# Second copies of 19 weight tiles, shared keys in the first products with v, normalizing on GpSimd

## The chip, the cores and the metric

The kernel runs on one core of a Trainium2 chip. A time is the device time of one execution in microseconds. The kernel before was timed three times: 958.98, 959.74 and 959.84 us, median 959.74.

The engines of a core are called here as in the profile: PE is TensorE (matmuls; PEld are its weight loads), DVE is VectorE, ACT is ScalarE, POOL is GpSimd, SP is SyncE, on whose queue this kernel issues all its transfers.

## The reference

```python
def _attn_ref(q, k, v):                  # each [8, 8, 576, 64], float32
    scores = matmul(q, k.T) / sqrt(64)
    rel = pos[:, None] - pos[None, :]
    mask_plain = (rel >= 0) & (rel < 32)                      # heads 0 to 3
    mask_dil = (rel >= 0) & (rel < 128) & (rel % 4 == 0)      # heads 4 to 7
    scores = where(mask, scores, -1e9)
    attn = exp(scores - max(scores))
    attn = attn / (sum(attn) + 1e-09)
    return matmul(attn, v)

def _moe_ref(x, w_in, w_out):            # [4608, 512], [512, 2048], [2048, 512]
    h = x @ w_in
    g = 0.5 * h * (1 + erf(h / sqrt(2)))
    return g @ w_out
```

x is the attention's result with a token's eight heads side by side. The weights reach the kernel as float64, the rest as float32.

## The kernel before, in words

**Tiling.** The 8 x 576 tokens are 16 chunks of 288 (`HALF`), half a batch entry each. Of a chunk, attention goes by four pairs of two heads: pairs 0 and 1 are plain, 2 and 3 dilated. The FFN follows with `h(c, f)`, the first product of chunk c for the f-th 128 of the 2048 hidden columns (`ffn_h`, L434, 12 matmuls of 288 columns), Gelu on ACT (L438), the split of g into a high and a low part (L441 on ACT, L443 on DVE), and the second product `o` (`ffn_o`, L448, 12 matmuls per f).

**Attention of a pair.** `scores` multiplies blocks of 32 queries with 64 keys each (L317). A dilated pair is laid out by residue of the position modulo 4, so its four row groups of 32 partitions hold one residue each, 72 queries in three blocks of 24 (computed 32 wide). A plain pair has three row groups. `lowest` adds the mask and finds the extremum (L329), `softmax` takes the exponential with its sum (L337; from chunk 2 on in other steps, `less`, `wide` and `sums`), `norm` divides by the sum (L357 to L366), `turn` transposes 32x32 squares (L374, and L379 from chunk 2 on), `av` multiplies with v (L403), and `xout` takes the result out of PSUM into a high part x (ACT, L421) and a low part (DVE subtraction, L423).

**Products with v.** In chunks 0 and 1 the 64 keys of a block are two halves of 32, a product of 32 rows each, added up in PSUM: 36 products for a plain pair, 48 for a dilated one. From chunk 2 on `turn` puts the two halves under each other, and one product has 64 rows; there are 18 and 24. A float32 product is two matmul records in the trace.

**Weights.** A tile of w_in or w_out is 128x512 float64, 512 KB, with the low word of each number first (`raw[:, :, 0]`) and the high word second. DVE splits it by integer passes. L243 shifts the low word right by 9, L245 ors the high word's last 9 bits on top (the low part's significand), L205 and L207 form a float32 from the high word (the high part, cut to 12 significand bits by the mask; ACT copies it, L217), L211 takes its exponent, and L255 multiplies the two to the low part. L205, L243 and L211 read one tile, the others two. The first tile is joined in another way (`w_join`, `w_join_pe`): TensorE adds the full value and minus the high part in PSUM (L233 to L235, with `ident` and `units`), and ACT copies the rest out (L237).

**Order.** Attention of chunks 0 to 2, all 32 weight tiles and the FFN of chunks 0 and 1 are ordered by `Plan`. It is a list scheduler that runs while the program is written: each job names what it comes after, which buffers it takes and gives back (`rings`), its rank and the guessed duration of each step, and the job that can start first is written next, with ranks for ties. The order that it writes is the order in each engine's queue. From chunk 3 on the attention steps stand at fixed places between the FFN's matmuls (`A_LOAD` to `A_N`, L598). Gelu of chunk 0 starts after all exponentials of chunk 1. Chunk 2's exponentials come after h(1, 15). The ring `wo` has 17 buffers for raw weight tiles, finished w_out tiles, and the keys and v of chunks 0 and 1.

Of the kernel before, what the change touches and what calls it, by code (L numbers as in the profile page):

```python
# [133 lines left out]
def attn_ffn(ctx: ExitStack, tc: tile.TileContext, qk_p, qk_d, v_p, v_d, w_in, w_out, outT):  # L134
# [28 lines left out]
    for k, d in ((PLAIN, KB), (DILATED, 2 * KB - QR)):  # L163
        for r in range(4):
            select(k, k, r, d, -1, 1, ALU.is_ge)
            select(k, k, r, WIN - d, 1, -1, ALU.is_gt)
        if k == PLAIN:
            select(PLAIN0, PLAIN, None, 0, 1, 0, ALU.is_ge)
            select(PLAIN0, PLAIN0, 0, -KB, 1, 0, ALU.is_ge)
            ident = const.tile([P, P], F32, name="ident")  # L170
            make_identity(nc, ident)
    select(DILATED0, DILATED, None, QR - 2 * KB, 1, 0, ALU.is_ge)
    select(DILATED1, DILATED, None, 2 * QR - 2 * KB, 1, 0, ALU.is_ge)
# [12 lines left out]
    units = []  # L186

    def w_units():

        yield {"DVE": 0.4}  # L190
        units.append(work.tile([P, 2, P], F32R, tag="go", name="units", bufs=3))
        for t, u in enumerate((1.0, -1.0)):
            nc.vector.tensor_scalar_mul(units[0][:, t], ident, u)
# [25 lines left out]
    def w_join(s, dst, i):  # L219

        raw = s["raw"]
        yield from w_top(s, 0x3FFFFFF8, gpool, "g", NF + 2)
        yield from w_exp(s)
        yield {"DVE": 0.6}
        g = s["g"] = gpool.tile([P, DM], F32R, tag="g", name="gw")
        nc.vector.scalar_tensor_tensor(g, raw[:, :, 0], 2.0 ** -52, raw[:, :, 1].bitcast(F32),
                                       op0=ALU.mult, op1=ALU.mult)

    def w_join_pe(s, dst, i):
        h, l = dst[i][:, 0], dst[i][:, 1]  # L230
        yield {"PE": 1.5}
        ps = ps_m.tile([P, 512], F32, tag="m", name="ps_w")
        nc.tensor.matmul(ps, ident, s["f"].bitcast(F32), start=True, stop=False)  # L233
        nc.tensor.matmul(ps, units[0][:, 1], h, start=False, stop=False)
        nc.tensor.matmul(ps, units[0][:, 0], s["g"], start=False, stop=True)  # L235
        yield {"ACT": 0.49}
        nc.scalar.copy(l, ps)  # L237
# [470 lines left out]
```

## Time and profile before

| | |
|---|---|
| median of three runs | 959.74 us |
| profiled execution, its own time | 960.52 us |
| its span | 958.7 us |
| mean granted TensorE clock | 0.982 |
| PE busy | 926.3 us (97%) |
| DVE busy | 486.9 us (51%) |
| ACT busy | 435.0 us (45%) |
| POOL busy | 6.2 us (1%) |
| DMA | 74.80 MB, mean 78 GB/s |

The page also has the span in 40 equal slices of some 24 us. A digit is the busy share of a slice in tenths:

```profile
PE   4589999999999999999999999999999999999998
DVE  6889996463533536244463534536353353634420
ACT  4644443554625345362443636245462534536240
POOL 2000000000000000000000000000000000000000
PEclk9589999999999999999999999999999999999999
DMA  9833323313040220403022040211304022040000
```

An idle engine is only worth something where another one waits for it, so the slices are read for the engine that is full, and the chain of waits for what it waited for. "issue" in the trace stands for time in which an engine waited for nothing that the profile shows.

### The profile page before, as it was taken

Reading aid. Unit: us, or ns where it says so; the run is one execution under the profiler, and the core shown is the slowest. Engines: PE = TensorE matmul, PEld = TensorE weight load, DVE = VectorE, ACT = ScalarE, POOL = GpSimd, SP = SyncE. Lnnn points to the kernel's source line nnn. Section 1 sums busy time; section 2 is a strip of 40 time slices with the busy share of each in tenths; the row PEclk is TensorE's granted clock in tenths of the full one; section 3 lists DMA queues with packets and bytes.
Section 4 is the critical chain, followed back from the end, with each engine's and each line's share of the span. In section 5 each row is a group of like instructions: output and inputs, shape, how many; then the busy total and the mean of one; then the engine's idle time right before and its main releaser. Section 6 shows DMA issues by size and latency. Waiting matters only on the chain.

```text
span 958.7 us, 27831 instructions
## 1 busy us (share of the span) xinstructions
PE 926.3 (97%) x11860; PEld 906.8 (95%) x11860; DVE 486.9 (51%) x1800; ACT 435.0 (45%) x1385; POOL 6.2 (1%) x27
## 2 busy tenths in 40 slices
PE   4589999999999999999999999999999999999998
PEld 2479999999999999999999999999999999999998
DVE  6889996463533536244463534536353353634420
ACT  4644443554625345362443636245462534536240
POOL 2000000000000000000000000000000000000000
PEclk9589999999999999999999999999999999999999
DMA  9833323313040220403022040211304022040000
GB/s 297 297 116 111 94 84 121 121 46 106 8 144 1 78 74 11 140 9 129 17 77 75 8 143 2 92 60 44 107 8 144 2 78 73 14 138 8 20 1 25
DMA packets 32252, 74.80 MB, mean 78 GB/s; under 512 B 3584, under 2 KB 11776, under 8 KB 32128
## 3 DMA queue, kind: packets, MB, share of 16 engines
q1 hardware_dynamic: 32128, 73.02, 23.1%
q8 instruction: 93, 1.52, 0.7%
q14 instruction: 31, 0.25, 0.1%
HBM read 63.57 MB, written 9.44 MB: 76 GB/s over the span
## 4 chain that ended last, share of the span: by engine, by line
PE 89%; DVE 7%; issue 2%; DMA 2%; SPq 0%; ACT 0%
PE ps_o L448 40%; PE ps_h L434 40%; PE px_a L403 4%; PE ps_a L317 3%; DVE cv L207 1%; DVE raw_w L245 1%; PE px L403 1%; DMA raw_qk<-qk_p 1%; DVE g L443 1%; DMA raw_qk<-qk_d 1%; PE ps_sc L317 1%; DVE raw_w L243 1%; DVE wout L255 1%; DVE cv L205 1%; DVE raw_w L211 1%
## 5 line engine op out<-in xcount | busy, mean ns | idle before, releaser
L448 PE MATMUL ps_o<-g,wout 128*128 128x288 f32 x3072 | 421.9, 296 | 0.9 <-DVE g L443 0.8
L448 PEld LDWEIGHTS ps_o<-g,wout 128*128 128x128 f32 x3072 | 410.4, 188 | 2.9 <-DVE g L443 1.7
L434 PE MATMUL ps_h<-xh,win 128*128 128x288 f32 x1920 | 390.5, 298 | 0.0
L434 PEld LDWEIGHTS ps_h<-xh,win 128*128 128x128 f32 x1920 | 308.8, 189 | 5.8 <-issue 3.2
L434 PE MATMUL ps_h<-xl,win 128*128 128x288 f32 x960 | 283.2, 295 | 0.0
L443 DVE TENSOR_TENSOR g<-gf,g 128x288 fp32r<-128x288 f32 x256 | 116.9, 457 | 261.5 <-ACT g L441 261.5
L438 ACT ACTIVATE gf<-ps_h 128x288 f32<-128x288 f32 x256 | 105.4, 412 | 293.1 <-PE ps_h L434 289.3
L434 PEld LDWEIGHTS ps_h<-xl,win 128*128 128x128 f32 x960 | 181.7, 189 | 0.0
L337 ACT ACTIVATE sm<-sm,st 96x64 f32<-96x64 f32 (+1 forms) x360 | 119.9, 334 | 14.4 <-DVE st L329 14.2
L441 ACT CAST g<-gf 128x288 fp32r<-128x288 f32 x256 | 110.7, 432 | 8.0
L421 ACT CAST xh<-px_a 128x288 fp32r<-128x288 f32 x52 | 27.8, 535 | 141.0 <-PE px_a L403 112.3
L379 DVE STREAM_TRANSPOSE turned<-sm 32x192 f32<-32x192 f32 x196 | 72.4, 369 | 5.3
L183 DVE COPY o_sb<-ps_o 128x288 f32<-128x288 f32 x58 | 26.4, 456 | 84.1 <-PE ps_o L448 82.0
L337 ACT ACTIVATION_READ_ACCUMULATOR sm<-sm,st 96x1 f32 (+1 forms) x360 | 67.4, 187 | 0.0
L423 DVE TENSOR_TENSOR xl<-px_a,xh 128x288 fp32r<-128x288 f32 x52 | 29.4, 565 | 58.5 <-ACT xh L421 58.1
L329 DVE CUSTOM_DVE_ANT_0 sm<-ps_a,masks 96x64 f32<-96x64 f32 (+1 forms) x312 | 46.9, 218 | 0.0
L403 PEld LDWEIGHTS px_a<-turned,v_all 64*64 64x64 f32 x2184 | 38.6, 134 | 4.2 <-issue 4.2
L403 PE MATMUL px_a<-turned,v_all 64*64 64x24 f32 (+1 forms) x2184 | 41.4, 218 | 0.0
L374 DVE STREAM_TRANSPOSE turned<-sm 96x384 f32<-96x384 f32 (+1 forms) x64 | 36.8, 575 | 2.0
L366 DVE TENSOR_TENSOR sm<-sm,st 96x384 f32<-96x384 f32 (+1 forms) x62 | 34.4, 555 | 1.8
L329 DVE DVE_READ_ACCUMULATOR2_ANT st<- 96x1 f32 (+1 forms) x384 | 30.9, 81 | 0.0
L317 PE MATMUL ps_sc<-raw_qk 64*32 64x64 f32 x504 | 11.3, 285 | 20.2 <-issue 9.9
(50 smaller groups left out, 377.1 us busy)
## 6 DMA issues: line engine op xcount, KB each, us to landing
raw_qk<-qk_d SPq DMA_DIRECT2D x32, 368.0 KB, 5.5
v_all<-v_p SPq DMA_DIRECT2D x28, 384.0 KB, 4.1
v_all<-v_d SPq DMA_DIRECT2D x28, 384.0 KB, 5.6
raw_qk<-qk_p SPq DMA_DIRECT2D x32, 304.0 KB, 3.5
outT<-o_sb SPq DMA_DIRECT2D x64, 144.0 KB, 1.8
raw_w<-w_in SPq DMA_DIRECT2D x16, 512.0 KB, 4.1
raw_w<-w_out SPq DMA_DIRECT2D x16, 512.0 KB, 4.4
v_sb<-v_d SPq DMA_DIRECT2D x4, 384.0 KB, 8.4
```

What stands on the lines that cost most here:

```text
L317: nc.tensor.matmul(s.sc[h][32 * r:32 * r + 32, u * 2 * KB:(u + 1) * 2 * KB], x[:, q0:q0 + 32], x[:, k0:k0 + 2 * KB], start=True, stop=True)
L329: nc.vector.tensor_tensor_reduce(out=s.sm[0:s.rows, i], in0=s.sc[h][0:s.rows, cols], in1=mask_of(s, u), scale=-SCALE, scalar=3.0e38, op0=A ...
L337: nc.scalar.activation(t, t, AF.Exp, bias=s.st[0:s.rows, 0, i:i + 1], scale=-1.0, accum_out=s.st[0:s.rows, 1, i:i + 1])
L366: nc.vector.tensor_mul(t, t, s.st[0:s.rows, 2].unsqueeze(2).broadcast_to((s.rows, 2 * NU, 2 * KB)))
L374: nc.vector.transpose(s.t[0:s.rows].rearrange("p i j b -> p (i j b)"), s.sm[0:s.rows].rearrange("p i k -> p (i k)"))
L379: nc.vector.transpose(s.t[32 * to:32 * to + 32, :, r % 2], s.sm[32 * r:32 * r + 32, :, j * KB:(j + 1) * KB])
L403: nc.tensor.matmul(px[h * D:(h + 1) * D, r - r0, u * s.nq:(u + 1) * s.nq], s.v[rows, u, j, h * D:(h + 1) * D], s.t[rows, 2 * u + h, j, 0:s ...
L434: nc.tensor.matmul(ps, wins[f][:, t, cc * P:(cc + 1) * P], xx, start=(n == 0), stop=(n == 3 * NC - 1))
L438: nc.scalar.activation(gf, ps, AF.Gelu)
L441: nc.scalar.copy(g[:, 0], gf)
L443: nc.vector.tensor_sub(g[:, 1], gf, g[:, 0])
L448: nc.tensor.matmul(ps, wouts[f][:, t, d * P:(d + 1) * P], gs[f][:, u], start=(f == 0 and n == 0), stop=(f == NF - 1 and n == 2))
```

## The change

**Second copies.** Of weight tiles 1 to 19 (`TWICE`; w_in and w_out alternate) SP brings a second copy into a buffer `mid`, shifted by two bytes (L188 of the changed kernel). Its 32-bit words then hold the middle of each number, and one mask (L215, one input) takes the place of the shift L243 and the two-input pass L245. Tiles 0 and 20 to 31 are split as tile 1 and later ones were before. The join on TensorE with `ident` and `units` goes. A ring of 18 buffers takes the copies in too, and in the planner a tile may be loaded 6 tiles ahead of its split instead of 5.

**Blocks of queries.** The queries of a row group now follow each other: 96 of a plain pair's, 72 of a dilated one's, in blocks of 32 (32, 32 and 8 of a dilated one's), and three masks do instead of five.

**Products with v in chunks 0 and 1.** v is laid out in four tiles of 32 keys for a row group. The keys of tile 1 are the second half of block 0 and the first half of block 1, so one product with 64 columns serves both; the same holds for tile 2. There are 24 products for a plain pair (12 with 64 columns, 12 with 32) and 32 for a dilated one. From chunk 2 on the products keep their number; a dilated pair's have 32, 32 and 8 columns.

**Normalizing.** In chunks 1 and 2 six GpSimd instructions on 64 columns each (L338) take the place of one DVE instruction on 384.

**The planner.** Its constants are others, and so is the order. Beside the host's layout of q, k and v the core of the diff is this (`KAPPA` and the ranks stand for the table):

```diff
-QP, QR = 32, 24
-KD = QD + 2 * KB - QR
-NKMAX = DIL * KD
+QP = HALF // 3
+KD = QD + KB
+NKMAX = 3 * KD + (NU + 1) * KB
...
-KAPPA, AHEAD, N_PE = 2e-05, 5, 1
-R_ATT, R_P = (0, 670, 480), 92
-R_F = 324
-R_A = {"load": 156, "v": -142, "scores": 58,
-       "exp": 32, "norm": 104, "t": -154, "av": -202, "x": -280, "less": -116, "sums": -72, "low": -106}
-R_W, R_WL = -448, -324
-R_H, R_O, R_E, R_O1 = 856, 1160, 1048, 644
+LATE, LATE_PE, COLD = 0.3, 0.3, 38
+KAPPA, AHEAD = 0.00011, 6
...
+TWICE = (1, 20)
...
+        if s["twice"]:
+            yield {"DMA": 1.4}
+            mid = wo.tile([P, 4 * DM], U16, tag="wo", name="mid_w")
+            nc.sync.dma_start(mid[:, 0:4 * DM - 2], src.bitcast(U16)[:, 1:4 * DM - 1])
+            s["mid"] = mid.bitcast(U32).rearrange("p (n t) -> p n t", t=2)[:, :, 0]
...
+        nc.vector.tensor_scalar(t, w1, 3, 0x3FFFF000, op0=ALU.logical_shift_left, op1=ALU.bitwise_and)
...
     def w_rest(s, dst, i):
 
         raw = s["raw"]
         yield {"DVE": 0.34}
+        if s["twice"]:
+            nc.vector.tensor_scalar(raw[:, :, 0], s["mid"], 0x01FFFFFF, None, op0=ALU.bitwise_and)
+            yield from w_top(s)
+            yield from w_exp(s)
+            return
         nc.vector.tensor_scalar(raw[:, :, 0], raw[:, :, 0], 9, None, op0=ALU.logical_shift_right)
         yield {"DVE": 0.6}
         nc.vector.scalar_tensor_tensor(raw[:, :, 0], raw[:, :, 1], 23, raw[:, :, 0],
                                        op0=ALU.logical_shift_left, op1=ALU.bitwise_or)
-        yield from w_top(s, 0x3FFFF000, work, "raw", 5)
+        yield from w_top(s)
...
-        nc.vector.scalar_tensor_tensor(dst[i][:, 1], raw[:, :, 0], 2.0 ** -43, raw[:, :, 1].bitcast(F32),
+        nc.vector.scalar_tensor_tensor(dst[i][:, 1], raw[:, :, 0], 2.0 ** (-36 if s["twice"] else -43),
+                                       raw[:, :, 1].bitcast(F32),
...
-        s.nr, s.nq = (3, QP) if s.plain else (DIL, QR)
+        s.nr, s.nq = (3, QP) if s.plain else (DIL, QD)
...
-            s.v = wo.tile([P, NU, 2, 2 * D], F32, tag="wo", name="v_sb")
+            s.v = wo.tile([P, NU + 1, 2 * D], F32, tag="wo", name="v_sb")
...
-                q0 = (u * s.nr + r) * QP if s.plain else r * QD + u * QR
-                k0 = HALF + ((u * s.nr + r) * QP if s.plain else r * KD + u * QR)
+                q0 = r * s.nq + u * KB
+                k0 = HALF + r * (QP if s.plain else KD) + u * KB
...
-        nc.vector.reciprocal(s.st[0:s.rows, 2], s.st[0:s.rows, 1])
-        e = yield {"DVE": 0.47, "ACT": 1.5}
-        t = s.sm[0:s.rows]
-        if e == "ACT":
+        nc.vector.reciprocal(st[:, 1], st[:, 1])
+        if s.c in (1, 2):
+            yield {"Pool": 2.2}
             for i in range(2 * NU):
-                nc.scalar.activation(t[:, i], t[:, i], AF.Copy, scale=s.st[0:s.rows, 2, i:i + 1])
+                nc.gpsimd.tensor_scalar(t[:, i], t[:, i], st[:, 1, i:i + 1], 1.0, op0=ALU.mult, op1=ALU.mult)
             return
-        nc.vector.tensor_mul(t, t, s.st[0:s.rows, 2].unsqueeze(2).broadcast_to((s.rows, 2 * NU, 2 * KB)))
+        yield {"DVE": 0.47}
+        nc.vector.tensor_mul(t, t, st[:, 1].unsqueeze(2).broadcast_to((s.rows, 2 * NU, 2 * KB)))
...
-        yield {"PE": (1.2 if s.plain else 1.6) if s.c < 2 else 0.9}
-        n = NU * s.nq
+        yield {"PE": (1.0 if s.plain else 1.3) if s.c < 2 else 0.9}
+        n = s.nq
         if s.c < 2:
             px = pools["px"].tile([P, 4, 512], F32, tag="px", name="px")
             s.px = [(px[:, 0:s.nr, 0:n], 0, s.nr)]
-        elif banks is None:
+
+            for m in (1, 3, 0, 2):
+                i0, k = (2 * (m - 1) * 2 + 1, 2) if 0 < m < NU else (0, 1) if m == 0 else (4 * (NU - 1) + 1, 1)
+                q0 = max(m - 1, 0) * KB
+                for r in range(s.nr):
+                    rows = slice(32 * r, 32 * r + 32)
+                    t = s.t[rows].rearrange("p i j b -> p (i j) b")
+                    for h in range(2):
+                        i = i0 + 2 * h
+                        nc.tensor.matmul(px[h * D:(h + 1) * D, r, q0:q0 + k * KB], s.v[rows, m, h * D:(h + 1) * D],
+                                         t[:, i:i + 3 * k - 2:3], start=m == 1, stop=m == 2)
+            return
+        if banks is None:
             px = [ps_m.tile([P, 512], F32, tag="m", name="px2").rearrange("p (a n) -> p a n", a=2) for _ in range(2)]
             s.px = [(px[0][:, :, 0:n], 0, 2), (px[1][:, 0:s.nr - 2, 0:n], 2, s.nr)]
         else:
-            at = s.p % 2 * NU * QP
+            at = s.p % 2 * QP
             s.px = [(banks.rearrange("p k (a n) -> p (k a) n", a=2)[:, 0:s.nr, at:at + n], 0, s.nr)]
         for u in range(NU):
+            b = min(KB, n - u * KB)
             for j in range(2):
-                for r in range(s.nr) if s.c < 2 else range(j, s.nr, 2):
+                for r in range(j, s.nr, 2):
                     px, r0, _ = s.px[-1] if r >= s.px[-1][1] else s.px[0]
+                    rows = slice(r // 2 * 64, r // 2 * 64 + 64)
                     for h in range(2):
-                        if s.c < 2:
-                            rows, first, last = slice(32 * r, 32 * r + 32), j == 0, j == 1
-                        else:
-                            rows, first, last = slice(r // 2 * 64, r // 2 * 64 + 64), True, True
-                        nc.tensor.matmul(px[h * D:(h + 1) * D, r - r0, u * s.nq:(u + 1) * s.nq],
-                                         s.v[rows, u, j, h * D:(h + 1) * D], s.t[rows, 2 * u + h, j, 0:s.nq],
-                                         start=first, stop=last)
+                        nc.tensor.matmul(px[h * D:(h + 1) * D, r - r0, u * KB:u * KB + b],
+                                         s.v[rows, u, j, h * D:(h + 1) * D], s.t[rows, 2 * u + h, j, 0:b],
+                                         start=True, stop=True)
```

TensorE from its first instruction, in the kernel before (`ps_sc` are scores, `px` products with v, x60 sixty in a row):

```order
L317 MATMUL ps_sc<-raw_qk 32x64 x60
L403 MATMUL px<-turned,v_sb 64x32 x36
L233 MATMUL ps_w<-cv,ident 128x512
L234 MATMUL ps_w<-win_148,units 128x512
L235 MATMUL ps_w<-gw,units 128x512
L317 MATMUL ps_sc<-raw_qk 32x64 x24
L403 MATMUL px<-turned,v_sb 64x32 x36
L317 MATMUL ps_sc<-raw_qk 32x64 x36
L403 MATMUL px<-turned,v_sb 64x24 x48
L317 MATMUL ps_sc<-raw_qk 32x64 x48
L403 MATMUL px<-turned,v_sb 64x24 x48
L317 MATMUL ps_sc<-raw_qk 32x64 x36
```

and in the changed kernel:

```order
L291 MATMUL ps_sc<-raw_qk 32x64 x84
L372 MATMUL px<-turned,v_sb 64x64 x6
L372 MATMUL px<-turned,v_sb 64x32 x12
L372 MATMUL px<-turned,v_sb 64x64 x6
L291 MATMUL ps_sc<-raw_qk 32x64 x18
...
L372 MATMUL px<-turned,v_sb 64x64 x8
L372 MATMUL px<-turned,v_sb 64x32 x16
L372 MATMUL px<-turned,v_sb 64x64 x8
L291 MATMUL ps_sc<-raw_qk 32x64 x48
```

The three instructions of the join (L233 to L235) are gone, scores of more pairs stand ahead of the first product with v, and a pair has 24 or 32 of these products (6, 12, 6 or 8, 16, 8) where it had 36 or 48. The 84 scores in a row are those of two plain and two dilated pairs, the 60 before those of two plain and one dilated.

SyncE's queue from its eighth entry on, in the kernel before (`qk_p` and `qk_d` bring the queries and keys of a plain and of a dilated pair, `v_p` and `v_d` the v):

```order
L198 DMA raw_w<-w_out 128x1024
L198 DMA raw_w<-w_in 128x1024
L280 DMA raw_qk<-qk_d 128x736
L287 DMA v_sb<-v_d 128x768
L198 DMA raw_w<-w_out 128x1024
L198 DMA raw_w<-w_in 128x1024
L280 DMA raw_qk<-qk_p 128x608
L287 DMA v_sb<-v_p 96x768
```

and in the changed kernel, from the same place (`mid_w` are second copies):

```order
L258 DMA raw_qk<-qk_d 128x728
L265 DMA v_sb<-v_d 128x512
L184 DMA raw_w<-w_out 128x1024
L258 DMA raw_qk<-qk_p 128x608
L265 DMA v_sb<-v_p 96x512
L188 DMA mid_w<-w_out 128x2046
L184 DMA raw_w<-w_in 128x1024
L258 DMA raw_qk<-qk_p 128x608
L188 DMA mid_w<-w_in 128x2046
L265 DMA v_sb<-v_p 96x512
```

The first `qk_p` in either piece holds the keys of chunk 1's first pair. Before, four weight tiles stand ahead of it in this piece; now one does, the keys of chunk 0's last pair have moved up past two, and second copies stand between the later keys.

VectorE where chunk 1's first pair is normalized, in the kernel before, with what each instruction waits for (`sm` the exponentials, `turned` their transposes):

```order
L366 TENSOR_TENSOR sm<-sm,st 96x384 [waits DVE_49]
L357 TENSOR_SCALAR st<-st 96x6 [waits Activation_49]
L245 SCALAR_TENSOR_TENSOR raw_w<-raw_w 128x512
L374 STREAM_TRANSPOSE turned<-sm 96x384 [waits DVE_49]
L359 RECIPROCAL st<-st 96x6 [waits DVE_49]
L205 TENSOR_SCALAR cv<-raw_w 128x512
L329 ISA sm,st<-ps_sc,masks 128x64 [waits PE_49]
L329 ISA st 128x1
```

and in the changed kernel, where its transposes wait for GpSimd (Pool):

```order
L403 TENSOR_TENSOR xl<-px,xh 128x4x72 [waits Activation_49]
L303 ISA sm,st<-ps_sc,masks 128x64 [waits PE_49]
L303 ISA st 128x1
...
L349 STREAM_TRANSPOSE turned<-sm 96x384 [waits Pool_49]
L231 SCALAR_TENSOR_TENSOR wout<-raw_w 128x512 [waits DMAHW2_49]
L349 STREAM_TRANSPOSE turned<-sm 96x384 [waits DVE_49,Pool_49]
L215 TENSOR_SCALAR raw_w<-mid_w 128x512 [waits DMAHW6_49,DMAHW1_49]
L303 ISA sm,st<-ps_sc,masks 128x64 [waits PE_49]
...
L332 TENSOR_SCALAR st<-st 128x6 [waits Activation_49]
L196 TENSOR_SCALAR cv<-raw_w 128x512
```

The normalizing instruction L366 has left VectorE. The first two transposes (L349) wait for GpSimd at the head of the queue, with scores of a dilated pair ahead of them and weight passes and the next pair's scores behind.

## Rows read from the trace of the kernel before

**Rows 1.** The page: engines (busy, share, instructions), and the queue that brings instructions (packets, MB, share).

```profile
PE 926.3 (97%) x11860; PEld 906.8 (95%) x11860; DVE 486.9 (51%) x1800; ACT 435.0 (45%) x1385; POOL 6.2 (1%) x27
q8 instruction: 93, 1.52, 0.7%
```

**Rows 2.** Stretches: length, busy us (xcount) of PE PEld DVE ACT POOL, PEclk, DMA, GB/s.

```profile
0.00:60.00 60.00, 31.53 (x1120) 26.00 (x1120) 45.20 (x232) 30.75 (x128) 6.20 (x27) 0.72 0.77 257
10.00:20.00 10.00, 6.92 (x244) 4.82 (x244) 8.55 (x45) 6.28 (x29) 0.00 (x0) 0.99 1.03 372
20.00:30.00 10.00, 3.68 (x172) 3.02 (x164) 8.40 (x40) 5.22 (x26) 0.00 (x0) 0.50 1.03 329
60.00:200.00 140.00, 139.13 (x1411) 136.79 (x1411) 109.97 (x293) 68.51 (x169) 0.00 (x0) 1.00 0.32 102
200.00:960.00 760.00, 755.66 (x9332) 744.03 (x9330) 331.74 (x1276) 335.79 (x1090) 0.00 (x0) 1.00 0.18 59
```

**Rows 3.** TensorE's timeline, 0 to 75 us: start, length, instructions xcount [idle before, releaser].

```profile
26.89 1.12 PE L317 MATMUL ps_sc<-raw_qk 64*32 64x64 f32 x41 [4.82 <-issue]
33.52 0.43 PE L403 MATMUL px<-turned,v_sb 32*64 32x24 f32 x10 [4.08 <-issue]
37.76 1.34 PE L403 MATMUL px<-turned,v_sb 32*64 32x24 f32 x77 [1.61 <-issue]
42.45 0.66 PE L317 MATMUL ps_sc<-raw_qk 64*32 64x64 f32 x23 [1.76 <-issue]
51.83 1.34 PE L403 MATMUL px<-turned,v_sb 32*64 32x24 f32 x96 [0.82 <-PE ps_h L434]
56.70 0.26 PE L317 MATMUL ps_sc<-raw_qk 64*32 64x64 f32 x1 [2.89 <-issue]
61.38 0.53 PE L434 MATMUL ps_h<-xh,win 128*128 128x288 f32 x2
```

**Rows 4.** DMA queues in the first 62 us.

```profile
q8 instruction: 9, 0.15, 1.0%
```

**Rows 5.** The chain of waits in the first 62 us: start, length, what.

```profile
10.88 10.29 DMA raw_qk<-qk_p
```

**Rows 6.** VectorE's timeline, 43 to 53 us.

```profile
43.80 0.54 DVE L349 TENSOR_TENSOR sm<-sm,st 96x384 f32<-96x384 f32 x1
44.27 0.68 DVE L245 SCALAR_TENSOR_TENSOR raw_w<-raw_w 128x512 uint32<-128x512 uint32 x1
49.52 0.41 DVE L243 TENSOR_SCALAR raw_w<-raw_w 128x512 uint32<-128x512 uint32 x1
49.86 0.44 DVE L443 TENSOR_TENSOR g<-gf,g 128x288 fp32r<-128x288 f32 x1
50.23 0.68 DVE L255 SCALAR_TENSOR_TENSOR win<-raw_w 128x512 fp32r<-128x512 uint32 x1
50.83 0.56 DVE L374 STREAM_TRANSPOSE turned<-sm 128x384 f32<-128x384 f32 x1
51.33 0.41 DVE L423 TENSOR_TENSOR x<-px,x 128x288 fp32r<-128x288 f32 x1
51.67 0.19 DVE L329 CUSTOM_DVE_ANT_0 sm<-ps_sc,masks 128x64 f32<-128x64 f32 x1
```

**Rows 7.** Timelines behind h(1, 15) and in a steady chunk, TensorE and VectorE.

```profile
144.09 10.87 PE L448 MATMUL ps_o<-g,wout 128*128 128x288 f32 x81
150.07 0.54 DVE L366 TENSOR_TENSOR sm<-sm,st 96x384 f32<-96x384 f32 x1
203.71 1.59 PE L403 MATMUL px_a<-turned,v_all 64*64 64x32 f32 x72
212.59 1.59 PE L403 MATMUL px_a<-turned,v_all 64*64 64x24 f32 x96
```

**Rows 8.** GpSimd's groups in the first 10 us: xcount | busy, mean ns | idle before.

```profile
L159 POOL TENSOR_SCALAR_AFFINE_SELECT masks<-masks 32x64 f32<-32x64 f32 x17 | 4.0, 233 | 1.0
L159 POOL TENSOR_SCALAR_AFFINE_SELECT masks<-masks 128x64 f32<-128x64 f32 x3 | 1.3, 444 | 0.1
```

More of the change, by code (lines that the diff above doesn't have):

```diff
@@ L6 @@
 from concourse._compat import with_exitstack
-from concourse.masks import make_identity
 F32 = mybir.dt.float32
@@ L133, in attn_ffn @@
 @with_exitstack
-def attn_ffn(ctx: ExitStack, tc: tile.TileContext, qk_p, qk_d, v_p, v_d, w_in, w_out, outT):
+def attn_ffn(ctx: ExitStack, tc: tile.TileContext, qk_p, qk_d, v_p0, v_d0, v_p, v_d, w_in, w_out, outT):
     nc = tc.nc
@@ L150, in upper_banks @@
         return upper.enter_context(tc.tile_pool(name=name, bufs=bufs, space=bass.MemoryType.PSUM))
-    masks = const.tile([P, 5, 2 * KB], F32, name="masks")
-    PLAIN, PLAIN0, DILATED, DILATED0, DILATED1 = range(5)
+    masks = const.tile([P, 3, 2 * KB], F32, name="masks")
+    ANY, PLAIN0, DILATED0 = range(3)
     def select(k, k0, r, base, step, mult, op):
@@ L162, in attn_ffn @@
     nc.gpsimd.memset(masks, 0.0)
[L163 to L173, printed above, removed]
+    for r in range(4):
+        select(ANY, ANY, r, KB, -1, 1, ALU.is_ge)
+        select(ANY, ANY, r, WIN - KB, 1, -1, ALU.is_gt)
+    select(PLAIN0, ANY, None, 0, 1, 0, ALU.is_ge)
+    select(PLAIN0, PLAIN0, 0, -KB, 1, 0, ALU.is_ge)
+    select(DILATED0, ANY, None, -KB, 1, 0, ALU.is_ge)
     pools = dict(px=upper_banks("ps_x", 1))
@@ L183, in copy @@
             nc.vector.tensor_copy(out, in_)
[L186 to L193, printed above, removed]
     def w_load(s, src, dst, i):
@@ L217, in w_high @@
         nc.scalar.copy(dst[i][:, 0], s["f"].bitcast(F32))
[L219 to L237, printed above, removed]
     def w_rest(s, dst, i):
@@ L296, in mask_of @@
     def mask_of(s, u):
-        first = s.c % 2 == 0
-        if s.plain:
-            k = PLAIN0 if first and u == 0 else PLAIN
-        else:
-            k = (DILATED0, DILATED1, DILATED)[u] if first else DILATED
+        k = ANY if s.c % 2 or u else PLAIN0 if s.plain else DILATED0
         return masks[0:s.rows, k]
@@ L324, in lowest @@
             s.sm = work.tile([P, 2 * NU, 2 * KB], F32, tag="sm", name="sm", bufs=5)
-            s.st = work.tile([P, 3, 2 * NU], F32, tag="st", name="st", bufs=5)
+            s.st = work.tile([P, 2, 2 * NU], F32, tag="st", name="st", bufs=5)
         cols = slice(u * 2 * KB, (u + 1) * 2 * KB)
@@ L414, in xout @@
                     s.x = tuple(xpool.tile([P, HALF], F32R, tag=n, name=n) for n in ("xh", "xl"))
[L415 to L420 removed]
+            h, l = (x.rearrange("p (r i) -> p r i" if s.plain else "p (i r) -> p r i", r=s.nr)[:, r0:r1] for x in s.x)
             nc.scalar.copy(h, px)
@@ L556, in attn_ffn @@
     k = attention_jobs(plan, 1, k, [])
-    attention_jobs(plan, 2, k, [("h", 1, GATE)] if GATE >= 0 else [])
-    plan.add(("units",), w_units(), [("exp", 0, 1)], ["go"], rank=R_W)
+    attention_jobs(plan, 2, k, [("h", 1, NF - 1)])
     for i in range(2 * NF):
         weight_jobs(plan, i)
-    plan.add(("units", "free"), free(), [("wlow", i) for i in range(N_PE)], [], ["go"], -100)
     plan.add(("x1", "free"), free(), [("h", 1, NF - 1)], [], ["big"], R_O1 - 200)
@@ L572, in attn_ffn @@
             plan.add(("h", c, f), ffn_h(xs[c], f, gs), [("x", c, p) for p in range(NPAIR)] +
-                     [("wlow", 2 * f), ("whigh", 2 * f)] + [("exp", c2, p) for c2 in range(1, 2 + (GATE == -1)) for p in range(NPAIR)] +
+                     [("wlow", 2 * f), ("whigh", 2 * f)] + [("exp", 1, p) for p in range(NPAIR)] +
                      ([("begun", ("h", c, f - 1))] if f else []),
@@ L698 @@
     arrays, args = {}, []
-    for name, a in (("qk_p", qk_p), ("qk_d", qk_d), ("v_p", vp), ("v_d", vd), ("w_in", wi), ("w_out", wo)):
+    for name, a in (("qk_p", qk_p), ("qk_d", qk_d), ("v_p0", vp0), ("v_d0", vd0), ("v_p", vp), ("v_d", vd), ("w_in", wi),
+                    ("w_out", wo)):
         a = np.ascontiguousarray(a)
```

79 lines of the change are left out of this document (39 added, 40 removed).

## The prediction

> **What bounds the kernel now.** I read the page first. TensorE is busy for 97% of the span [rows 1], so a change can pay only where TensorE is idle or slow. The table of stretches says where. From 200 us on it is busy for 755.66 of 760 us at a granted clock of 1.00, and 60 to 200 is as full. [...] The first 60 us, in which chunks 0 and 1 go through attention, are all there is to win.
>
> What holds TensorE there? The timeline of its own instructions answers [rows 3]. It is idle for 4.82 us before 26.89, for 4.08 before 33.52, 1.61 before 37.76, 1.76 before 42.45 and 2.89 before 56.70, and each time the releaser is "issue": nothing that the profile shows. Counted in matmul records, these stops stand at 347, 474, 599, 725 and 1107: multiples of some 127 apart. The instruction queue explains the number. It moved 93 packets, 1.52 MB, in the span [rows 1], which is 16 KB each. TensorE has 11860 matmuls and as many weight loads, 23720 instructions, 255 to a packet, or 128 matmuls. In the first 62 us 9 such packets came [rows 4], and some 1216 matmuls ran, 9.5 packets' worth. So I read "issue" as TensorE waiting for its next block of instructions. From 26.89 to 56.70 us six blocks went by: 4.97 us for each, 39.2 ns for each small matmul, while one takes 14.0 ns where nothing holds it (96 in 1.34 us at 51.83) [rows 3].
>
> [...]
>
> VectorE is the second bound: 45 of the first 60 us busy, and 110 of the next 140 [rows 2]. The marker for both engines is the fourth first-product block of chunk 0, h(0,3). It starts at 61.38 [rows 3], and from it on TensorE is full. At that point the same work is done before and after the change: all of attention of chunks 0 and 1, the scores of chunk 2, and h(0,0) to h(0,2). What the change does to its start, it does to the end.
>
> **The small matmuls.** A float32 product is two matmul records. The first products with v of chunks 0 and 1 go from 36 to 24 products for a plain pair and from 48 to 32 for a dilated one: over four pairs of each 336 become 224, that is 224 records fewer. The join's four go too. So h(0,3) stands after 988 records instead of 1216. At 39.2 ns each that is **8.9 us**. If blocks were not what holds TensorE, 228 x 14.0 ns = 3.2 us. I take 8.9, because the stops recur at the count that the packets give.
>
> **The loads ahead of attention.** Transfers run full from 10 to 30 us (372 GB/s in 10 to 20) [rows 2], and the chain of waits passes 10.29 us of waiting for the keys of chunk 1's first pair [rows 5]. Up to and with these keys the SP queue has 5.69 MB before and 3.65 MB after (by the shapes in its order, 4 bytes an element, 2 in a second copy): three weight tiles moved behind them, and the four tiles of v ahead of them lost a third. For the last keys of chunk 1 it is 8.26 and 7.45 MB, two second copies included. So the first keys come 2.04 / 0.372 = 5.5 us sooner, the last ones 2.2 us. The last ones count; I take **2.0 us**, bounds 0 and 5.5. The other second copies (9.96 MB in all, 26.8 us of transfers) stand behind most keys. Up to the fourth w_in tile and its copy SP has 12.75 MB to bring: with 2.4 MB in the first 10 us and 0.372 MB per us from there it has landed at 38 to 40 us, 10 us before it is needed. A copy that starts two bytes off is in no row. At half the rate, the six copies ahead would make that 48 us, just in time; at a quarter, h(0,3) would be some 16 us late.
>
> **VectorE.** Start-to-start prices from [rows 6]: a weight pass with one input 0.34, with two 0.60, normalizing 0.47, a transpose 0.50, a g 0.37, a subtraction for x 0.34. For the last pass on the fourth w_in tile, which ends at 50.8 us, VectorE has 38.0 us of work by these prices, so 12.8 us were idle. After the change it has one single-input pass more in front of this tile (+0.34), four two-input passes fewer (-2.4), two normalizations fewer (-0.95), by the new order two transposes (+1.0), two subtractions (+0.7) and one g (+0.37) more, and no units (-0.27): 36.8 us. With the same idle time the tile is ready at 49.6 us. To the last tile 18 two-input passes fewer and the rest make 11.7 us (126.2 to 114.5); behind h(0,3) that is slack, not time, since TensorE is the full engine there.
>
> So h(0,3) is due at 61.4 - 8.9 - 2.0 = 50.5 by TensorE's blocks and not before 49.6 by VectorE; I take 50.5, **10.9 us** sooner.
>
> **What is lost.** From chunk 2 on, a dilated pair's products with v go from three blocks of 24 columns to 32, 32 and 8. The records: 72 matmuls of 32 columns in 1.59 us, 22.1 ns each; 96 of 24 in 1.59, 16.6 [rows 7]: by columns, 0.69 ns each. Then 8 columns cost 5.5 ns and the sum would not change. But the products of rows 3 took 14.0 ns with the same 24 columns on half the rows: a floor. With 14.0 for the short ones two pairs cost 64 x 22.1 + 32 x 14.0 = 1.86 us instead of 1.59: 0.27 us per chunk, 14 chunks, **3.8 us**. Bounds: 0, and 5.0 if a short one costs 16.6. I take the floor, the nearest row of such a size.
>
> **Normalizing on GpSimd.** No row has this operation. The nearest are its mask selects on 64 columns: 233 ns on 32 partitions, 444 on 128 [rows 8]. Six make 1.4 to 2.7 us for a pair; I take 2.2, towards the larger tile. In chunk 1 the transposes that wait for it have some 3 us of other VectorE work ahead of them: hidden. If not, they hold VectorE's queue: behind the first stand the scores of chunk 1's last pair, x of chunk 0's last pair and weight passes. In chunk 2 the four pairs go one after another: the first is normalized from 150.07, 6 us after h(1,15) [rows 7], so the last is done 6 + 8.8 us after it and turned 1.8 later, at 16.6 (0.50 and parts of some 0.35). TensorE has 126 second products (81 in 10.87 us [rows 7]) and three products with v, 19.5 us, before it asks for it. Hidden up to 2.9 us a pair.
>
> Sum: 10.9 - 3.8 = 7.1 us off the profiled execution's 960.52, 953.4. That execution stands 0.8 us above the median of 959.74, so by the median **952.6 us**.
>
> **Rivals.**
> [...]
>
> *VectorE sets the pace and idles longer*, with its new waits for GpSimd. 5 us more puts h(0,3) at 54.6, 6.8 us gained, and the time at 956.7, or 952.9 with the short matmuls free. For it: its margin here is 0.9 us. [...]
>
> *Slower: GpSimd becomes the chain.* At 0.95 us an instruction a pair takes 5.7. In chunk 2 the last pair is then due 6 + 22.8 + 1.8 = 30.6 us after h(1,15), 11.1 us after TensorE asks. In chunk 1 VectorE's queue waits for it as well, and of the 10.9 us some 3 are left: 959.7 - 3 + 3.8 + 11.1 = 971.6. It decides from about 4.5 us a pair, where the loss in chunk 2 (6.3) and the short matmuls eat what is left. Against it: the 444 ns.
>
> *More*: the early keys' 5.5 us are on the path and short matmuls are free, 8.9 + 5.5 = 14.4, 945.3; VectorE would have to idle 4 us less, as it may with its scores earlier.
>
> **How the numbers follow.** The forecast gets 0.50; with the bounds on loads and short matmuls it lies between 948 (VectorE's 49.6, short ones free) and 955.8 (nothing from the loads, 5.0 for the short ones). VectorE the pace 0.23, blocks hidden 0.11, more 0.08, slower 0.08 (slow copies are in it). The range for 8 in 10 is 947 to 958. A measurement of this kernel can tell 0.2%, 1.9 us, from no change: below 957.8 it is faster. Of the two smaller gains some 0.08 lands within 0.2%, nearly all of it where blocks are hidden. Faster 0.84, same 0.08, slower 0.08.
>
> **What would show it.** h(0,3) near 50 us, with stops by "issue" again some 127 matmuls apart and two fewer of them before it; at the same counts but short, the fetch is not the pace. VectorE without long waits for GpSimd before a transpose. Weight passes that wait for the second copy would show the copies slow. In a steady chunk the dilated products with v at 1.86 us. TensorE waiting before the products with v after h(1,15), GpSimd instructions near 1 us, or passes of VectorE stretched beside them would make the prediction wrong.

## The result and the profile after

| | before | after |
|---|---|---|
| median (runs) | 959.38 us (4) | 949.14 us (947.95 to 950.46, 4) |
| ratio | 1 | 0.9891, 95% interval 0.988 to 0.9903 |
| profiled execution, its span | 960.52 us, 958.7 | 950.46 us, 948.7 |
| forecast | | 952.6 us, range 947 to 958 |

The changed kernel is 10.2 us faster; 7.1 were forecast. The page after answers [rows 1]. There are 228 matmuls fewer and two instruction packets fewer; POOL has the normalizing:

```profile
PE 920.4 (97%) x11632; PEld 902.8 (95%) x11632; DVE 474.7 (50%) x1775; ACT 431.5 (45%) x1372; POOL 21.1 (2%) x64
...
q8 instruction: 91, 1.49, 0.7%
```

The stretches (columns as in [rows 2]):

```profile
0.00:60.00 60.00, 35.12 (x1028) 30.16 (x1029) 45.66 (x232) 31.45 (x124) 14.14 (x40) 0.94 0.93 337
10.00:20.00 10.00, 5.95 (x240) 4.81 (x246) 9.16 (x63) 8.18 (x47) 0.00 (x0) 1.00 1.04 347
20.00:30.00 10.00, 4.09 (x174) 3.09 (x170) 8.15 (x42) 6.67 (x32) 4.84 (x10) 1.00 1.04 373
...
40.00:50.00 10.00, 7.21 (x223) 6.22 (x226) 8.97 (x41) 4.93 (x9) 1.27 (x3) 0.83 1.03 405
...
60.00:200.00 140.00, 140.00 (x1402) 138.47 (x1401) 104.83 (x290) 67.75 (x181) 6.97 (x24) 1.00 0.39 133
```

TensorE still works for only 4.09 of the 10 us from 20 to 30. The transfers now run full up to 50 us (share 1.03, 405 GB/s from 40 to 50 us, where it was 0.44 and 124 before) and at 0.65 from 50 to 60. From 60 to 200 us TensorE is busy without a gap, where it had 139.13 of 140.

TensorE's timeline, its stops by "issue" and h(0,3), as in [rows 3]:

```profile
17.21 0.87 PE L291 MATMUL ps_sc<-raw_qk 64*32 64x64 f32 x32 [1.55 <-issue]
...
24.73 1.18 PE L372 MATMUL px<-turned,v_sb 32*64 32x64 f32 x53 [1.43 <-issue]
...
30.91 0.64 PE L291 MATMUL ps_sc<-raw_qk 64*32 64x64 f32 x22 [3.32 <-issue]
...
36.10 0.47 PE L372 MATMUL px<-turned,v_sb 32*64 32x64 f32 x4 [2.53 <-DVE st L332]
37.02 1.13 PE L372 MATMUL px<-turned,v_sb 32*64 32x64 f32 x44 [0.45 <-issue]
...
43.37 0.53 PE L291 MATMUL ps_sc<-raw_qk 64*32 64x64 f32 x28 [1.17 <-issue]
...
49.85 0.43 PE L291 MATMUL ps_sc<-raw_qk 64*32 64x64 f32 x25 [1.63 <-issue]
...
54.71 0.52 PE L414 MATMUL ps_h<-xh,win 128*128 128x288 f32 x2
```

Counted in matmul records the stops stand at 220, 347, 474, 600, 728 and 855; before, they stood at 347, 474, 599, 725 and 1107. The work and its order are others, and the stops keep their counts. But the blocks have become slower: from 24.73 to 49.85 four went by, 6.28 us each, against 4.97 before.

The prediction passes over two stops by "issue" of the kernel before. One of 0.45 us stands at record 220, a count like the others. One of 1.24 us ends at 19.17, at record 244, which is no such count: a transposition of VectorE (L374) had ended at 19.07. So the label alone doesn't tell a wait for instructions from a wait for VectorE; the count does.

**Where 10 us came from,** by the two profiled executions. These stand 1.1 and 1.3 us above their medians, and the four runs of the changed kernel lie within 2.5 us, so a time such as h(0,3) is known from one trace to some 2 us (an estimate).

- h(0,3) starts at 54.71 instead of 61.38: **6.7 us**.
- From there to the first scores of chunk 3's second half (182.05 before, 173.33 after) TensorE issues the same 852 large matmuls. It needs 120.67 us before and 118.62 after: **2.05 us**. Before, it stopped for VectorE's low parts of g. The long stop of this stretch stands in the timeline, and the weight loads' waits, 1.7 of the 2.05 us, sum it up (total, times, longest):

```profile
85.40 1.99 PE L448 MATMUL ps_o<-g,wout 128*128 128x288 f32 x13 [0.78 <-DVE g L443]
```
```profile
PEld ps_o L448 <- DVE g L443: 1.7, 4, 1.0
```

After the change this stretch has no such wait. What made up the rest, the rows don't tell.

- A steady chunk lasts 56.77 us instead of 56.89, over 13.6 chunks **1.6 us**. The same products with v of chunk 15, of before and after, against chunk 3's at 203.71 [rows 7] and 194.95:

```profile
886.44 1.59 PE L403 MATMUL px_a<-turned,v_all 64*64 64x32 f32 x72
```
```profile
194.95 1.59 PE L388 MATMUL px_a<-turned,v_all 64*64 64x32 f32 x72
...
203.80 1.58 PE L388 MATMUL px_a<-turned,v_all 64*64 64x32 f32 x96
...
876.23 1.59 PE L388 MATMUL px_a<-turned,v_all 64*64 64x32 f32 x72
```

Twelve chunks take 682.73 us before and 681.28 after. The row at 203.80 is that of the two dilated pairs with their blocks of 32, 32 and 8: 1.58 us, where the blocks of 24 took 1.59 [rows 7]. The three terms make 10.3 us; 0.3 goes back behind the last matmul.

GpSimd's normalizing, in chunk 1 (24 to 43 us) and in chunk 2 (130 to 150), busy us and mean ns:

```profile
L338 POOL TENSOR_SCALAR sm<-sm,st 128x64 f32<-128x64 f32 x12 | 5.6, 493 | 5.0 <-DVE st L334 5.0
L338 POOL TENSOR_SCALAR sm<-sm,st 96x64 f32<-96x64 f32 x12 | 5.5, 481 | 21.0 <-DVE st L334 21.0
```
```profile
L338 POOL TENSOR_SCALAR sm<-sm,st 128x64 f32<-128x64 f32 x12 | 3.5, 320 | 95.7 <-DVE st L332 95.7
L338 POOL TENSOR_SCALAR sm<-sm,st 96x64 f32<-96x64 f32 x12 | 3.5, 316 | 0.0
```

### The profile page after: what moved, and what is told of

Read it like the earlier page. It is cut to its first block, busy times and chain, and to the rows that moved or that the text cites. A ratio compares the mean times of both kernels' runs of the same rounds, so it can differ in the third digit from the quotient of the medians.

```text
span 948.7 us, 27417 instructions
## 1 busy us (share of the span) xinstructions
PE 920.4 (97%) x11632; PEld 902.8 (95%) x11632; DVE 474.7 (50%) x1775; ACT 431.5 (45%) x1372; POOL 21.1 (2%) x64
## 4 chain that ended last, share of the span: by engine, by line
PE 95%; DMA 3%; issue 0%; SPq 0%; DVE 0%
PE ps_h L414 44%; PE ps_o L428 44%; PE px_a L388 4%; PE ps_a L291 3%; DMA raw_w<-w_in 1%; DMA mid_w<-w_in 1%; DMA raw_qk<-qk_d 1%; PE px L372 0%; PE px L388 0%; PE ps_sc L291 0%; SPq L265 0%; SPq L258 0%; DVE o_sb L178 0%; SPq L184 0%; DVE st L332 0%
## 5 line engine op out<-in xcount | busy, mean ns | idle before, releaser
L403 DVE TENSOR_TENSOR xl<-px_a,xh 128x288 fp32r<-128x288 f32 x52 | 29.5, 568 | 58.2 <-ACT xh L401 57.8
L303 DVE CUSTOM_DVE_ANT_0 sm<-ps_a,masks 96x64 f32<-96x64 f32 (+1 forms) x312 | 47.0, 218 | 0.0
L349 DVE STREAM_TRANSPOSE turned<-sm 96x384 f32<-96x384 f32 (+1 forms) x64 | 36.9, 576 | 8.9 <-POOL sm L338 4.2
L388 PE MATMUL px_a<-turned,v_all 64*64 64x32 f32 (+1 forms) x2184 | 41.2, 217 | 0.0
L341 DVE TENSOR_TENSOR sm<-sm,st 96x384 f32<-96x384 f32 (+1 forms) x56 | 31.1, 556 | 1.9
L303 DVE DVE_READ_ACCUMULATOR2_ANT st<- 96x1 f32 (+1 forms) x384 | 31.3, 81 | 0.0
L332 DVE TENSOR_SCALAR st<-st 96x6 f32<-96x6 f32 (+1 forms) x64 | 10.3, 164 | 39.6 <-ACT sm L311 38.8
```

Source lines behind the costliest of these rows:

```text
L303: nc.vector.tensor_tensor_reduce(out=s.sm[0:s.rows, i], in0=s.sc[h][0:s.rows, cols], in1=mask_of(s, u), scale=-SCALE, scalar=3.0e38, op0=A ...
L341: nc.vector.tensor_mul(t, t, st[:, 1].unsqueeze(2).broadcast_to((s.rows, 2 * NU, 2 * KB)))
L349: nc.vector.transpose(s.t[0:s.rows].rearrange("p i j b -> p (i j b)"), s.sm[0:s.rows].rearrange("p i k -> p (i k)"))
L388: nc.tensor.matmul(px[h * D:(h + 1) * D, r - r0, u * KB:u * KB + b], s.v[rows, u, j, h * D:(h + 1) * D], s.t[rows, 2 * u + h, j, 0:b], sta ...
L403: nc.vector.tensor_sub(l, px, h)
```

## The experiments

Ratios are to the kernel before on the same chip, with 95% intervals; the changed kernel has 0.9891 (0.988 to 0.9903). The theory: ahead of h(0,3) TensorE waits for blocks of instructions. The rivals: VectorE, the keys, or GpSimd.

**E1, shared keys undone.**

```diff
-   matmul(px[.., q0:q0 + k * KB], v[rows, m, ..], t[:, i:i + 3 * k - 2:3], start=m == 1, stop=m == 2)
+   for b in range(k):
+       matmul(px[.., q0 + b * KB:q0 + (b + 1) * KB], v[rows, m, ..], t[:, i + 3 * b],
+              start=m == 1 and b == 0, stop=m == 2 and b == k - 1)
```

> The changed kernel with each 64-column product with v of chunks 0 and 1 split into two of 32 columns: 36 and 48 products for a pair again, 224 matmul records more ahead of h(0,3), the written order of every engine else the same. Theory (TensorE waits for blocks of some 127 records, one per 6.28 us while the transfers run full): 1.76 blocks more, h(0,3) 10 to 11 us later than 54.7, time 958 to 960. Rival (a small matmul costs its 14.0 ns and the fetch has slack): 3.1 us later, 952. Second rival (VectorE's passes or the landing of keys set h(0,3)): under 1 us, 949 to 950.

Measured: 952.99 us, 0.9933 (0.992 to 0.9947), h(0,3) at 58.80. The 224 records cost 3.9 us, far less than the theory's 10 to 11 and near the first rival's number, but not by its mechanism: the stops are there, and longer.

```profile
23.39 0.20 PE L373 MATMUL px<-turned,v_sb 32*64 32x32 f32 x1 [3.74 <-issue]
...
29.60 0.63 PE L373 MATMUL px<-turned,v_sb 32*64 32x32 f32 x5 [3.17 <-issue]
...
33.54 1.61 PE L373 MATMUL px<-turned,v_sb 32*64 32x32 f32 x70 [1.03 <-issue]
...
39.62 1.41 PE L373 MATMUL px<-turned,v_sb 32*64 32x32 f32 x52 [0.45 <-issue]
```

By "issue" TensorE lost 12.5 us up to h(0,3), in the changed kernel 9.6. The blocks took 6.21, 3.94 and 6.08 us here. Beside the quick one the transfers moved 177 GB/s, beside the two others 400 and 341. So a record seems to have no fixed price, but one that depends on the transfers beside it; E2 puts that to the test.

**E5, half of these products left out.**

```diff
-   for m in (1, 3, 0, 2):
+   for m in (1, 3):
```

> The changed kernel with half of the products with v of chunks 0 and 1 left out (12 and 16 for a pair instead of 24 and 32, so x of these chunks is not the reference's): 224 matmul records fewer ahead of h(0,3), the written order else the same. With 224 more, 3.9 us were lost. Theory A (blocks of instructions hold TensorE there, at 6 us each while transfers run full): 4 to 8 us sooner than 949, 941 to 945. Theory B (blocks and VectorE hold it in turns; what a block gives back, VectorE keeps): 1 to 3 us sooner, 946 to 948. Rival (VectorE alone by now): within 1 us.

Measured: 945.27 us, 0.9846 (0.9832 to 0.9861): 3.9 us sooner, at the edge of A and B. TensorE's waits up to 48 us say why no more came (total, times, longest):

```profile
PE ps_sc L291 <- DMA raw_qk<-qk_p: 10.4, 5, 3.7
PE px L372 <- DVE st L332: 3.0, 1, 3.0
PE px L372 <- DVE xl L403: 2.4, 2, 1.7
...
PE ps_sc L291 <- issue: 1.0, 1, 1.0
```

The stops by "issue" are gone but for 1.0 us, and waits for VectorE and keys have taken their place. From 20 to 48 us VectorE is busy for 25.30 of 28 us (22.72 in the changed kernel).

**E6, less work for VectorE.**

```diff
-   nc.vector.scalar_tensor_tensor(t, w1, 0xC0000000, t, ...)
+   if not 1 <= s["i"] < 8:
+       nc.vector.scalar_tensor_tensor(t, w1, 0xC0000000, t, ...)
```

> The changed kernel without the two-input or pass (L198) of weight tiles 1 to 7, whose values are then not the reference's: 7 passes of 0.60, 4.2 us of VectorE's work less ahead of h(0,3) or beside it, the written order else the same. Theory A (blocks alone hold h(0,3)): within 1 us of 949. Theory B (in turns; four normalizations on VectorE, 1.9 us of work, cost 2.1): 2 to 3 us sooner, 946 to 947. Rival (VectorE alone): 4 us sooner, 945.

Measured: 950.12 us, 0.9903 (0.9887 to 0.9919): nothing gained. The stops stay, 6.9 us of them:

```profile
PE ps_sc L292 <- issue: 6.0, 4, 2.8
PE px L373 <- DVE xl L404: 4.0, 2, 2.3
...
PE px L373 <- issue: 0.9, 2, 0.7
```

VectorE is busy for 19.60 us from 20 to 48 us, 3.1 less than in the changed kernel, and nothing comes of it.

E5 and E6 together: in the changed kernel the blocks hold the head, and VectorE, with the keys, is next. Its last pass on the fourth w_in tile ends at 50.56 in the changed kernel, 4.15 us before h(0,3), and in E5 at 47.05, 0.9 us before it.

**E2, the second copies' transfers left out.**

```diff
-   mid = wo.tile(...); nc.sync.dma_start(mid[...], src...)
-   s["mid"] = mid...[:, :, 0]
+   s["mid"] = s["raw"][:, :, 0]
```

> The changed kernel without the transfers of the second copies; the mask pass reads the first copy instead, so the low parts of 19 weight tiles are not the reference's. Every other instruction and its place in each queue are the same; 9.96 MB of transfers are gone. Theory (an instruction block waits behind the data transfers, which run full to 50 us in the changed kernel): the blocks come about every 4.5 to 5 us instead of 6.28, so that over the four from 24.7 to 49.9 us some 5 us go, h(0,3) at 48 to 50, time 943 to 945. Rival (VectorE or something else sets that pace): the blocks keep to 6 us, within 1 us of 949.

Measured: 944.88 us, 0.9846 (0.9833 to 0.986): 4.3 us sooner, as the theory had it; h(0,3) at 48.88. Its stops by "issue" from 20 us on:

```profile
22.11 1.19 PE L370 MATMUL px<-turned,v_sb 32*64 32x64 f32 x53 [1.69 <-issue]
...
26.04 0.65 PE L289 MATMUL ps_sc<-raw_qk 64*32 64x64 f32 x22 [1.39 <-issue]
...
32.01 1.60 PE L370 MATMUL px<-turned,v_sb 32*64 32x64 f32 x48 [3.30 <-issue]
...
39.05 0.53 PE L289 MATMUL ps_sc<-raw_qk 64*32 64x64 f32 x29 [0.96 <-issue]
...
43.88 0.43 PE L289 MATMUL ps_sc<-raw_qk 64*32 64x64 f32 x25 [1.31 <-issue]
```

All but the one at 32.01 stand at a block's count. That one stands at record 596, ahead of the first product with v of chunk 1, and is VectorE's: `px` has one buffer, and the subtraction that reads the pair before out of it ends 0.1 us earlier.

```profile
31.25 0.67 DVE L401 TENSOR_TENSOR xl<-px,xh 128x288 fp32r<-128x288 f32 x1
```

The other stops, with one at 15.44, sum to 6.8 us, where the changed kernel has 9.6. The four blocks from record 347 to 855 take 21.77 us instead of 25.12. The first and the last of them hold no such wait for VectorE; here they are in E2, then in the changed kernel (columns as in [rows 2]):

```profile
22.11:26.04 3.93, 2.54 (x127) 2.19 (x127) 3.74 (x20) 3.31 (x14) 3.75 (x8) 1.00 0.89 284
39.05:43.88 4.83, 3.52 (x128) 3.03 (x127) 4.83 (x22) 1.82 (x4) 0.00 (x0) 1.00 0.60 235
```
```profile
24.73:30.91 6.18, 2.86 (x128) 2.29 (x128) 4.77 (x24) 4.47 (x21) 5.50 (x12) 1.00 1.03 401
43.37:49.85 6.48, 4.86 (x127) 4.26 (x128) 6.25 (x25) 2.46 (x5) 0.00 (x0) 0.74 1.03 404
```

VectorE had the same passes, so its own work did not set that pace. The 4.3 us are not the blocks' alone: record 347 comes 2.6 us sooner, and chunk 1's last keys land at 22.15 instead of 26.67.

**E4, no second copies** (`TWICE = (0, 0)`), **E7 and E8, later ones** (`(5, 24)` and `(9, 28)`).

> The changed kernel without second copies: all tiles are split by the shift and the two-input pass, the planner orders anew. Theory (copies slow the blocks, 5 us, while their passes save VectorE about 1 us ahead of h(0,3) and up to 2.1 us of stalls on g behind it): h(0,3) 4 us sooner, then 1 to 2 us lost behind it, 946 to 947. Rival (transfers don't slow the blocks; the copies are worth what VectorE saves): 1 to 3 us later, 950 to 952.

> The changed kernel with second copies of tiles 5 to 23 instead of 1 to 19, planned anew: the transfers of copies begin behind the keys of chunk 1. Theory (their transfers between 9 and 40 us cost 4.3 us through the instruction blocks and the keys; the two-input passes of tiles 1 to 4 give back 4 x 0.26 = 1.0 us of VectorE): 946 to 948. Rival (VectorE's early passes decide): 949.5 to 951.

> The changed kernel with second copies of tiles 9 to 27, planned anew. Theory (early copies cost more than they give, later ones keep VectorE ahead of g behind h(0,3)): 946 to 948. Rival (VectorE's early passes decide, 8 x 0.26 = 2.1 us more of them): 950 to 952.

Measured: 950.21 us, 0.9902 (0.9889 to 0.9916); 949.02, 0.9886 (0.9872 to 0.9901); 949.47, 0.9891 (0.9874 to 0.9907). None can be told from the changed kernel. In E4 the profile still has 6.1 us by "issue", but not at a block's count: 1.9 us at record 400 and 4.2 at 596, and each ends 0.1 us after an instruction of VectorE (L303 at 25.46, the transposition L349 at 35.22). E7 has its two at the same records. VectorE is busy for 19.46 of the 20 us from 20 to 40 in E4, and TensorE waits another 8.8 us for its x parts up to 53.7. So without early copies VectorE holds the head in the blocks' place. The copies' whole effect is 1.1 us by E4, not clear of noise. It looks as if their transfers take back what they spare VectorE; the order is another, so this is argued and not shown. None brought the gain that the theory expected: E4 came out by its rival, E7 and E8 between the two.

**E3, normalizing on VectorE again.**

```diff
-   if s.c in (1, 2):
+   if False:
```

> The changed kernel with normalizing on VectorE in chunks 1 and 2 as before the change; the planner orders anew. Theory (blocks set h(0,3), GpSimd's part is hidden and so is VectorE's): within 1.5 us of 949. Rival (VectorE is the pace there, 4 x 0.47 us come back on it): 1.9 us later or more, 951 and above. Second rival (the 2.6 us that VectorE waits for GpSimd were on the path): 1 to 2.6 us sooner, 947.

Measured: 951.25 us, 0.9913 (0.9899 to 0.9926): 2.1 us later, the first rival's number, at the edge of what can be told. It was not sooner, as the second rival had it. The planner's order changed with it, so how much of it is VectorE's work stays open.

**E9, fewer tiles ahead** (`AHEAD` 4 for 6), **E10, E7 with GpSimd in chunk 0's dilated pairs too** (`or (s.c == 0 and s.p >= 2)`).

> The changed kernel, planned anew with a weight tile allowed 4 instead of 6 tiles ahead of its split: up to chunk 1's keys SP's queue is the same, behind them fewer transfers wait in it. Theory (transfers that are not needed yet fill the queues to 62 us and slow the instruction blocks before h(0,3)): 1 to 3 us sooner than 949, 946 to 948. Rival (the transfers ahead of 40 us are the same, and VectorE then waits for tiles): 949 to 951.

> Second copies of tiles 5 to 23 (949.0 us by itself, with VectorE full from 20 to 30 us and few stops by issue) and normalizing on GpSimd for the two dilated pairs of chunk 0 as well, planned anew. Theory (VectorE holds that version's head, so 2 x 0.47 us taken off it show): 0.5 to 2 us sooner than 949.0, 947 to 948.5. Rival (chunk 0's pairs wait 2.7 us each for GpSimd instead of 0.47 for VectorE, on the path to the first x): 1 to 2 us later, 950 to 951.

Measured: 950.19 us, 0.9914 (0.9901 to 0.9928), and 951.48, 0.9919 (0.9906 to 0.9933): both went the rivals' way, E10 beyond its 1 to 2 us. No version that does all the work is clearly faster than the changed kernel.

**E11, the buffers where they were before.**

```diff
-   masks = const.tile([P, 3, 2 * KB], ...)     wo: bufs=NF + 2, Plan(dict(wo=NF + 2, ...))
+   masks = const.tile([P, 7, 2 * KB], ...)     wo: bufs=NF + 1, Plan(dict(wo=NF + 1, ...))
```

> The changed kernel with its buffers at the addresses of the kernel before (the masks' buffer made 1024 bytes larger, the ring of weight tiles 17 instead of 18, planned so). A steady chunk lasts 56.90 us in the kernel before and 56.77 in the changed one and in each experiment on it. If the place of the buffers makes the difference, a chunk lasts 56.90 here; if the blocks of 32, 32 and 8 queries or something else in the steady part does, it stays at 56.77. The head may come out up to 2 us later for the smaller ring.

Measured: 949.61 us in one run. Twelve steady chunks last from 194.10 to 875.39, 56.77 us each: by this one trace the places of the buffers are not the reason.

**E12, the kernel before without its join on TensorE** (`N_PE = 0`).

> The kernel before with its first weight tile split by VectorE's passes like the others instead of joined on TensorE; the written order of the rest is the same. TensorE has 4 records fewer, VectorE some 0.7 us of passes more (0.94 more, units' 0.27 less). Theory (the stops by issue recur at the same counts, and what TensorE loses at the join, about 2.6 us of waits between 14 and 17 us, is hidden before the first of them): within 1 us of the kernel before. Rival (these waits are on the path to h(0,3)): 1.5 to 2.6 us sooner.

Measured: 959.09 us, 0.9992 (0.9983 to 1.0001): no difference. (Its profiled execution, 958.10 us, was the fastest of eleven; h(0,3) stands at 58.95 in it.) Two of its stops stand where [rows 3] has them, at 33.52 and 37.76, to 0.01 us:

```profile
33.51 0.41 PE L403 MATMUL px<-turned,v_sb 32*64 32x24 f32 x5 [4.05 <-issue]
...
37.76 1.28 PE L403 MATMUL px<-turned,v_sb 32*64 32x24 f32 x71 [1.62 <-issue]
```
```profile
20.00:30.00 10.00, 3.78 (x190) 3.25 (x182) 9.34 (x49) 5.54 (x27) 0.00 (x0) 1.00 1.03 320
```

Four records fewer, other passes on VectorE, a granted clock of 1.00 from 20 to 30 us instead of 0.50 [rows 2], and the same two values from 30 to 40: none of them moves these two stops. That excludes the clock as their reason.

## Why the prediction was right, and where its terms were not

The direction and the place (the first 60 us, instruction blocks) were right, and 949.14 lies in the range. But h(0,3) came 4.2 us later than forecast, and the sum came out through errors that partly cancel, which is luck.

**The blocks: right mechanism, wrong size.** The step "At 39.2 ns each that is 8.9 us" failed. From record 347 to h(0,3) TensorE needs 34.5 us before and 30.0 after, 4.5 less, and E1 and E5 price 224 records at 3.9 us in either direction, 17 ns each. The 4.97 us of a block came from a stretch in which transfers thinned out from 40 us on (124 GB/s from 40 to 50 us); the changed kernel keeps them full (405 GB/s), and a block takes 6.28. The four blocks from record 347 on so lost 4 x 1.31 = 5.2 us of the two blocks saved (9.9). And VectorE and the keys stand close behind (E5): another 224 records fewer gave 3.9 us and no more.

**The second copies.** They came in time, as forecast (VectorE waited for one of them once, for 1.1 us), and two bytes off cost no rate: 405 GB/s from 40 to 50 us, against 372 from 10 to 20 in the kernel before [rows 2]. That their transfers slow the blocks was in no term. E2 puts what they cost in all, by the blocks and by later keys, at 4.3 us.

**The loads.** The landings came as forecast: the keys of chunk 1's first pair at 15.02 instead of 21.17 us, 6.2 sooner (5.5 forecast), its last keys at 26.67 instead of 28.91, 2.2 sooner (2.2 forecast). What they gave no run measures by itself. Record 347 is reached at 24.73 instead of 26.89, 2.2 us sooner against 2.0 forecast, but the work ahead of it is not the same.

**VectorE.** Its part ahead of h(0,3) was second, as said: the fourth w_in tile was ready at 50.56, forecast 49.6. "behind h(0,3) that is slack, not time" was wrong: there, 2.05 us went, most of it waits for g. The row of 60 to 200 us that showed TensorE 0.87 us short of full was read as full.

**The short matmuls.** The step "I take the floor" of 14.0 ns failed: 3.8 us forecast, nothing measured. With 22.1 ns for 32 columns (rows of 1.59 us for 72) the 32 short ones took 1.58 us - 64 x 22.1 ns = 0.17 us, 5.2 ns each: by columns, here down to 8.

**GpSimd.** A pair took 2.8 us in chunk 1 (2.2 forecast, hidden up to 2.9 in chunk 2) and 1.75 in chunk 2. VectorE waited for it 2.6 us in three pieces; nothing shows them on the path (E6 took more work off VectorE and gained nothing, and E3, without these waits, was not sooner). The rival "slower" was far off.

**The steady chunks.** Their 1.6 us were not forecast. In the middle of the trace (300 to 800 us) the start-to-start time of two first-product matmuls is 132.7 ns instead of 133.2 in the mean. All twelve kernels with the new blocks of queries show it, E12 with the old ones doesn't, and E11 speaks against the places of the buffers. What does it is open.

So 10.9 - 3.8 was forecast, and 6.7 + 2.05 + 1.6 came. Of the other cases, "blocks hidden" (3.2 us in place of 8.9) falls with the counts: the stops stand at 220 to 855 again, some 127 apart. "VectorE sets the pace" had h(0,3) at 54.6, and 54.71 is nearly its number, but its mechanism falls with E6; it is the limit behind.

Undone one at a time, the shared keys are worth 3.9 us (E1), GpSimd's part 2.1, at the edge of what can be told (E3), the second copies 1.1, not clear of noise (E4), and leaving out the join gave the kernel before nothing (E12). With the steady chunks' 1.6 that is 8.7 of the 10.2 us. The planner's new order has a part in these numbers that no run separates.

## What to carry to other kernels

When an engine stops at equal counts of its own instructions, with nothing to wait for, count its instruction packets: fewer instructions there can be worth more than their own time (17 ns a record here, against 14.0). Check what ended just before such a stop, since a wait for another engine can carry the same label (1.24 us at record 244 here, 3.30 in E2). Price such a stop only beside the same load of transfers (a block took 6.28 us here where they ran full and 4.97 where they thinned out), and ask of every added transfer whether such a stretch lies beside it. Once the first limit is moved, the next one, here VectorE 4 us behind, caps the gain: price it before the sum is made.
